# Low parts of an expert's weights on VectorE, two weight chunks loaded earlier, first loads in another order

## The chip, the core and the metric

The kernel runs on one core of one Trainium2 chip. The metric is the device time of one execution in microseconds (us). A core has TensorE (PE: matrix products and transposes), VectorE (DVE), ScalarE (ACT), GpSimd (POOL) and SyncE (SP), each with its own instruction queue that runs in order. Queues meet at semaphores. SyncE issues nearly all loads here; a load stands in SyncE's queue until its buffer is free, and everything behind it stands with it.

## The reference

Three stages, all in fp32, with 2 batches of 768 rows, 8 heads of 64:

```python
# 1: windowed attention, 8 global and 96 local columns, with a slope per head
scores = scale * (q @ k.T) + bias; scores = where(keep, scores, -1e9)
x = softmax(scores) @ v                       # (2, 768, 512)
# 2: a mixture of 8 experts, one expert for each row
logits = x @ w_gate; gate = sigmoid(x @ w_local)
e = argmax(logits) if s == 0 or gate < 0.5 else expert of the row before
out = p[e] * (relu(x @ w1[e]) @ w2[e])        # w1: 512x1024, w2: 1024x512 for each expert
# 3: a mix with the row before
xk = mu_k*x + (1-mu_k)*x_prev;  xr = mu_r*x + (1-mu_r)*x_prev
k = relu(xk @ w_k);  r = sigmoid(xr @ w_r);  out = r * ((k*k) @ w_v)
```

## The kernel before, in words

Each fp32 product is made of three matrix products of rounded halves: an operand is split into a high part, `hi = round(x)`, written by ScalarE, and a low part, `lo = x - hi`, and TensorE adds `hi*hi + lo*hi + hi*lo` (`mm3`, which the trace shows as L598 to L600). So every weight chunk of 128x1024 numbers passes through a load, two ScalarE copies (`whi`) and a subtraction (`wlo`).

The order of the instructions on every engine is that of the Python code; nothing is scheduled by a planner. Hand-written tables say how many steps of a background queue run behind each foreground step.

*Attention.* At the start the two integers `n_global` and `n_local` are loaded (`scalars_load`, L136), cast (L141), and turned into one mask and distance table for each head (`table`, L518; heads above 3 on GpSimd), popped from a list `tq`. Then the pairs of heads run in a pipeline: scores (`emit_qk`, L734), the row minimum (`emit_min`, L746, which needs the tables), the exponential (`emit_exp`, L756), transposes, products with `v`. Dummy products (`warm`, L896) fill some of TensorE's gaps.

*Routing* runs beside the last heads and in a tail after them: gate logits, the switch `ab` (L187 to L211), products that spread it over a row (L221), a scan over the rows (`er`, L232), the sort by expert (L241 to L260), and scatters of the rows from GpSimd into the tensor `xs` (L253). The first expert's work on the rows known early (`fill`, a generator) is the foreground of that tail. Its weights are split by `w_hi(0, c)` and `w_lo(0, c)`, called from `w_next` in between. For chunks 4 to 6 the low part is one GpSimd instruction of 128x1024 (L567), for chunk 7 half of it is on VectorE (L571).

*Experts 1 to 7.* Raw weight chunks live in a ring of four buffers (`wraw`), which x0, the rows of the first expert's later tile, also shares. While the first expert ends, chunks 0 and 1 of expert 1 are loaded and split (`w1q`). From chunk 2 on, loads come from a list `lq`: after each low part (`w_lo_all`, L591) `pump` issues the next load of the list. Token tiles (`x_load`, tiles `xn`, L1120) are in the same list, before the weight chunk with number 7.

*Stage 3's weights* arrive as words that VectorE has to decode. `dec_load` (L1171) loads one piece of 512 KB into one of two `dw` buffers on SyncE's queue; `dec` decodes it in four VectorE steps (L449, L452, L454, L456). The generator `background` runs these steps between the experts' own. Stage 3 follows at about 354 us.

Of the kernel before, what the change touches and what calls it, by code (L numbers as in the profile page):

```python
# [52 lines left out]
class Net:  # L53
# [76 lines left out]
    def scalars_load(self, c):  # L130
        nc = self.nc
        self.raw = raw = c.tile([P, 4], I32, name="n_raw")
        for j, nm in enumerate(("n_global", "n_local")):
            src = self.i[nm].bitcast(I32)
            src = bass.AP(tensor=src.tensor, offset=src.offset, ap=[[0, P], [1, 2]])
            nc.sync.dma_start(out=raw[:, 2 * j:2 * j + 2], in_=src)  # L136

    def scalars(self, c):
        nc, raw = self.nc, self.raw
# [360 lines left out]
    def tables0(self, keep, pool):  # L500
        nc = self.nc
        r0 = self.rel[:, CP:W]
        m0 = pool.tile([P, P], F32, name="m0")
        d0 = pool.tile([P, P], F32, name="d0")
        nc.vector.tensor_scalar(m0, self.colg, self.ng, NEG, op0=ALU.is_ge, op1=ALU.mult)
        nc.vector.tensor_scalar(d0, r0, self.nl, None, op0=ALU.min)
        nc.vector.scalar_tensor_tensor(m0, r0, self.nl, m0, op0=ALU.is_ge, op1=ALU.mult)
        self.tb0 = keep.tile([P, H, P], F32, tag="tb0", bufs=1, name="tb0")

        return [lambda h=h: self.table(self.tb0[:, h, :], d0, m0, h, h > 3) for h in range(H)]  # L510

    def table(self, dst, dist, mask, h, pool):
        nc, s = self.nc, 2.0 ** -(h + 1)
# [19 lines left out]
def build(ctx, tc, ins, out):  # L533
# [21 lines left out]
    def w_hi(r, c):  # L555
        raw = raws[r, c]
        hi = wp.tile([P, 1024], F32R, tag="whi", bufs=10, name=f"whi{r}_{c}")
        for s in range(2):
            sl = slice(s * 512, s * 512 + 512)
            nc.scalar.activation(out=hi[:, sl], in_=raw[:, sl], func=ACTF.Copy)  # L560
        whl[r, c] = hi

    def w_lo(r, c, pool_lo=False):
        raw, hi = raws.pop((r, c)), whl[r, c]
        lo = wp.tile([P, 1024], F32R, tag="wlo", bufs=10, name=f"wlo{r}_{c}")
        if pool_lo:
            nc.gpsimd.tensor_tensor(lo, raw, hi.bitcast(F32), op=ALU.subtract)  # L567
        else:
            for s, eng in ((0, nc.vector), (1, nc.gpsimd)):
                sl = slice(s * 512, s * 512 + 512)  # L570
                eng.tensor_tensor(lo[:, sl], raw[:, sl], hi[:, sl].bitcast(F32), op=ALU.subtract)  # L571
        whl[r, c] = (hi, lo)

    def w_hi1(r, c, s, dve=False):
# [14 lines left out]
    def w_lo_all(r, c):  # L589
        hi, lo = whl[r, c]  # L590
        nc.vector.tensor_tensor(lo, raws.pop((r, c)), hi.bitcast(F32), op=ALU.subtract)  # L591

    def w_split(r, c, pool_lo=False):
        w_hi(r, c)
        w_lo(r, c, pool_lo)

    def mm3(out_, ah, al, bh, bl, first, last):
        nc.tensor.matmul(out_, lhsT=ah, rhs=bh, start=first, stop=False)  # L598
# [126 lines left out]
    def emit_qk(pair):  # L725
        t, h = pair
        j = t % NT
        p = h // 2
        c0 = 0 if j else CP
        N = W - c0  # L730
        k0 = cols(t) + P - N
        ps = [n.bank("S", 2) for _ in range(2)]
        for a in range(2):
            nc.tensor.matmul(ps[a][:, 0:N], lhsT=qz[t % 2][a * HD:(a + 1) * HD, p, :], rhs=strip[a * HD:(a + 1) * HD, p, k0:k0 + N], start=True, stop=True)  # L734
        Ss[pair] = ps
# [144 lines left out]
            step(mid=early_start)  # L880

    with tc.manual_schedule():
        for g in range(2):
            load("k", 0, g)
            load("q", 0, g)
            if g == 0:
                n.scalars_load(n.const)
        n.setup()
        peb = [ap.tile([P, 2 * P], F32, name=f"peb{i}") for i in range(4)]
        qz = [ap.tile([P, PAIRS, P], F32, name=f"qz{i}") for i in range(2)]  # L890
# [3 lines left out]
        def warm(k, m=512):  # L894
            for _ in range(k):
                nc.tensor.matmul(n.bank("O", 2)[:, 0:m], lhsT=n.warm[:, 0:P], rhs=n.warm[:, 0:m], start=True, stop=True)  # L896
# [6 lines left out]
        n.scalars(n.const)  # L903
        tq = n.tables0(ap, tp) + n.tables(ap, tp)
        first = first_half(0)
        for _ in range(9):
            tq.pop(0)()
        for nm, a in ("k1", "q1", "v0", "v1"):
            load(nm, int(a))
# [45 lines left out]
        wseq = []  # L955
        for c in range(NIN, 8):
            wseq.append(lambda c=c: w_hi(0, c))
            wseq.append(lambda c=c: w_lo(0, c, c < 7))

        def w_next():  # L960
            if wseq:
# [4 lines left out]
        first_half(1)  # L966
        del kn[0], qn[0]
        emit_min(0, pairs[0])
        emit_qk(pairs[1])
        warm(NDUM[1], 64)  # L970
        for i in range(NP_ + 3):
            t, h = pairs[i] if i < NP_ else (NTT + (i - NP_) // 4, 2 * ((i - NP_) % 4))
# [119 lines left out]
        for k, _ in enumerate(fl):  # L1092
            if k > 6 and w1q:
                c, s = w1q.pop(0)
                if s < 2:
                    w_hi1(1, c, s)
                else:
                    w_lo1(1, c, s - 2)
    astack.close()
    zp = wstack.enter_context(tc.tile_pool(name="zp", bufs=1))  # L1100
    mstack = ExitStack()
# [288 lines left out]
    with tc.manual_schedule():  # L1390
        lq = []

        for r in range(1, E):
            if r == 1:
                lq.append(lambda r=r: x_load(r))
            else:
                lq.append(lambda r=r: ereg(r))
            for c in range(0 if r > 1 else 2, 8):
                if c == 7 and r < E - 1:
                    lq.append(lambda r=r: x_load(r + 1))  # L1400
                lq.append(lambda r=r, c=c: w_load(r, c))

        def pump(m=1):
            for _ in range(m):
                if lq:
                    lq.pop(0)()

        sq = [(r, c, s) for r in range(1, E) for c in range(0 if r > 1 else 2, 8) for s in range(3)]
        sq += [(E, c, s) for c in WORD for s in range(4)]

        def w3_split(c, s):
            if s == 0:
                w_hi1(E, c, 0)
                return
            if s == 1 and c in DVEHI:
                nc.vector.tensor_copy(whl[E, c][0][:, 512:], raws[E, c][:, 512:])
            elif s == 1:
                w_hi1(E, c, 1)
            else:
                w_lo1(E, c, s - 2)  # L1420

        def W_(m=1):
            for _ in range(m):
                if sq:
                    r, c, s = sq.pop(0)
                    if r == E:
                        w3_split(c, s)
                    elif s < 2:
                        w_hi1(r, c, s)
                    else:  # L1430
                        w_lo_all(r, c)
                        pump(1 if c != 5 else 3)

        pump(1)
        dec_load(PIECES[0])
        pump(1)
        dec_load(PIECES[1])
        pump(1)
        hn = ztile([P, 2, D], F32, "hn")
        eh = [xtile([P, KF, P], c, f"eh{c}") for c in "hl"]  # L1440
        for u in xs_tile(0, xhl0[:, 0], xhl0[:, 1], [hn[:, s, :] for s in range(2)], eh, BASES[0] + 2 * P):
            W_(W0[u])
            B_(B0[u])
            if u == 0:
                pump(1)
            if u in X1_AT:
                x_hi(1, X1_AT.index(u))
            if u - 1 in X1_AT:
                x_lo(1, X1_AT.index(u - 1))
        for r in range(1, E - 1):  # L1450
            nx = len(TILES[r + 1])
            for f in range(KF):
                l1m(r, f)
                if f in (3, 4, 5) and f - 3 < nx:
                    x_lo(r + 1, f - 3)
                if f in (2, 3, 4) and f - 2 < nx:
                    x_hi(r + 1, f - 2)
                W_((1, 2, 2, 1, 1, 1, 1, 1)[f])
                B_(BL1[f])
            nt = len(TILES[r])  # L1460
            for i in range(nt):
                ps = n.bank("O", 2)
                m = nrow(r, i)
                if i == 2:
                    src, a = [tuple(h[:, f, 0:m] for h in h3["hl"]) for f in range(KF)], 0
                else:
                    src, a = [hs[r, f] for f in range(KF)], i
                for f in l2_mm(r, ps, a, src, m):
                    if f == 0 and i == 0:
                        W_(2)  # L1470
                    elif (f < 6 if i else nt < 3 and f < 7):
                        W_(1)
                    if f % 2 == 0:
                        B_(1)
                y_out(rp, ps, BASES[r] + TILES[r][i] * P, m)

        r = E - 1
        for i in range(2):
            hn = wp.tile([P, 2, D], F32, tag="wraw", bufs=4, name=f"hn{i}")
            eh = [xtile([P, KF, P], c, f"eh{c}{i}") for c in "hl"]  # L1480
            xh, xl = (x[:, :, i * P:(i + 1) * P] for x in xhl[r])
            for u in xs_tile(r, xh, xl, [hn[:, s, :] for s in range(2)], eh, BASES[r] + i * P):
                if i:
                    early(u)
                W_(W7[i][u])
                B_(1)
            if i == 0:
                for _ in bg:
                    pass
                n.small_w3(rp)  # L1490
                early(-1)
        stage3()
# [214 lines left out]
```

## Time and profile before

| | before |
|---|---|
| median of three runs | 551.25 us (551.23 to 552.83) |
| profiled execution | 555.6 us, its span 553.8 us |
| TensorE busy | 530.4 us, 96% |
| VectorE busy | 372.8 us, 67% |
| ScalarE busy | 289.5 us, 52% |
| GpSimd busy | 149.1 us, 27% |
| mean granted clock | 0.973 of full |

The span is the time from the first to the last instruction that the profiler saw. Times of single instructions are all from this one execution. A row of a timeline has the start in us, the duration in us, the engine, the line of the kernel, the operation with its output and inputs, and a count; in brackets stands the idle time of the engine just before it and what ended it. TensorE is nearly always busy, so a saving on another engine counts only where TensorE stands behind it. The granted clock of 1.0 stands for 2.4 GHz and 0.5 for 1.2 GHz.

### The profile page before, as it was taken

The numbers are of one execution on the slowest core, as the hardware profiler recorded it, in microseconds if no ns is written. First come the engines' busy times: TensorE is split into PE (matmuls) and PEld (weight loads), VectorE is DVE, ScalarE is ACT, GpSimd is POOL, SyncE is SP. The second block draws the span as 40 slices with busy tenths as digits, with TensorE's granted clock in tenths as the row PEclk, the third lists the DMA queues.
The fourth block names the chain that finished last, engine by engine and source line by source line (L and its number), as shares of the span: only waits on it lengthen the run. The fifth ranks groups of instructions, "written<-read, shape, count | busy, mean of one in ns | idle before, by whom it ended". The sixth has DMA issues, their size and how long they took to land.

```text
span 553.8 us, 9727 instructions
## 1 busy us (share of the span) xinstructions
PE 530.4 (96%) x3285; PEld 450.9 (81%) x3285; DVE 372.8 (67%) x937; ACT 289.5 (52%) x709; POOL 149.1 (27%) x234
## 2 busy tenths in 40 slices
PE   6999999989789799999999999999999999999995
PEld 4787887777668698889898998778898989898885
DVE  6688889786663388588989979869744344444311
ACT  4787888866424544556565655557433332424130
POOL 4443353473530000000000000043535261716130
PEclk9799999987989999999999999999999999999999
DMA  6875374833114984758789897211101010110101
GB/s 127 209 168 144 76 169 105 239 103 126 41 39 141 315 289 154 283 181 273 251 301 339 286 354 247 89 59 57 58 20 43 34 40 38 39 40 1 39 2 43
DMA packets 74137, 76.99 MB, mean 139 GB/s; under 512 B 50496, under 2 KB 50752, under 8 KB 74080
## 3 DMA queue, kind: packets, MB, share of 16 engines
q1 hardware_dynamic: 68464, 63.28, 37.5%
q0 software_dynamic: 1920, 6.29, 3.5%
q10 hardware_dynamic: 3696, 6.72, 3.2%
q8 instruction: 28, 0.46, 0.3%
q14 instruction: 29, 0.24, 0.2%
HBM read 63.27 MB, written 13.01 MB: 138 GB/s over the span
## 4 chain that ended last, share of the span: by engine, by line
PE 69%; DVE 18%; DMA 5%; issue 3%; ACT 2%; SPq 1%; POOL 0%; DVEq 0%; ACTq 0%; POOLq 0%
PE O L598 10%; PE O L600 9%; PE O L599 9%; PE S L598 6%; PE S L600 6%; PE S L599 6%; PE S L734 4%; DVE wlo L591 4%; DMA wraw<-in_moe_w_dram 3%; PE PT L600 3%; PE PT L599 3%; PE PT L598 3%; PE T L680 2%; PE R L181 2%; PE PT L765 2%
## 5 line engine op out<-in xcount | busy, mean ns | idle before, releaser
L582 ACT ACTIVATE whi<-wraw 128x512 fp32r<-128x512 f32 x116 | 67.2, 623 | 18.8 <-DMA wraw<-in_moe_w_dram 11.5
L591 DVE TENSOR_TENSOR wlo<-wraw,whi 128x1024 fp32r<-128x1024 f32 x54 | 65.8, 1219 | 11.4 <-ACT whi L582 11.2
L1270 ACT ACTIVATE rl<-S 128x256 f32<-128x256 f32 x48 | 18.5, 385 | 80.4 <-PE S L600 80.3
L598 PE MATMUL S<-xkh,whi 128*128 128x256 f32 x192 | 54.5, 284 | 0.4 <-DVE sq L1272 0.4
L599 PE MATMUL S<-xkl,whi 128*128 128x256 f32 x192 | 53.6, 279 | 0.6 <-DVE xkl L1248 0.6
L600 PE MATMUL S<-xkh,wlo 128*128 128x256 f32 x192 | 53.6, 279 | 0.0
L1280 POOL TENSOR_TENSOR kl<-sq,kh 128x256 fp32r<-128x256 f32 x40 | 31.9, 807 | 80.2 <-ACT kh L1279 80.2
L1225 POOL MEMSET strip<- 128x4 f32 x2 | 0.2, 115 | 192.4 <-DVE wlo L587 192.4
L1310 DVE TENSOR_TENSOR o<-O,sig 128x512 f32<-128x512 f32 (+1 forms) x13 | 8.5, 651 | 61.3 <-PE O L600 34.5
L746 DVE CUSTOM_DVE_ANT_0 sc<-S,tb 128x232 f32<-128x232 f32 (+1 forms) x96 | 32.3, 373 | 21.0 <-PE S L734 14.1
L756 ACT ACTIVATE peb<-sc,nm 128x232 f32<-128x232 f32 (+1 forms) x96 | 44.2, 464 | 1.9 <-DVE nm L746 1.9
L598 PE MATMUL O<-whi,kh 128*128 128x512 f32 (+1 forms) x104 | 39.2, 377 | 0.0
L599 PE MATMUL O<-wlo,kh 128*128 128x512 f32 (+1 forms) x104 | 39.2, 377 | 0.0
L600 PE MATMUL O<-whi,kl 128*128 128x512 f32 (+1 forms) x104 | 39.2, 377 | 0.0
L598 PE MATMUL O<-whi,hh 128*128 128x512 f32 x96 | 38.0, 396 | 0.0
L599 PE MATMUL O<-wlo,hh 128*128 128x512 f32 x96 | 37.9, 395 | 0.0
L600 PE MATMUL O<-whi,hl 128*128 128x512 f32 x96 | 37.9, 395 | 0.0
L775 ACT ACTIVATE pth<-PT 128x512 fp32r<-128x512 f32 (+1 forms) x48 | 26.9, 561 | 20.5 <-PE PT L767 15.2
L1272 DVE SCALAR_TENSOR_TENSOR sq<-S,rl 128x256 f32<-128x256 f32 x48 | 19.9, 420 | 25.8 <-ACT rl L1270 25.0
L599 PEld LDWEIGHTS S<-xkl,whi 128*128 128x128 f32 x192 | 36.1, 188 | 1.0 <-DVE xkl L1248 0.8
L598 PEld LDWEIGHTS S<-xkh,whi 128*128 128x128 f32 x192 | 36.0, 187 | 0.9 <-DVE sq L1272 0.6
L734 PE MATMUL S<-strip,qz 64*128 64x232 f32 (+1 forms) x192 | 33.7, 419 | 2.9 <-DVE nm L746 2.8
(351 smaller groups left out, 1607.7 us busy)
## 6 DMA issues: line engine op xcount, KB each, us to landing
wraw<-in_moe_w_dram SPq DMA_DIRECT2D x64, 512.0 KB, 5.2
ys<-yo ACTq DMA_DIRECT2D x17, 256.0 KB, 4.1
dw<-in_moe_w_k_dram SPq DMA_DIRECT2D x8, 512.0 KB, 4.9
dw<-in_moe_w_v_dram SPq DMA_DIRECT2D x8, 512.0 KB, 5.7
xn<-xs SPq DMA_DIRECT2D x14, 256.0 KB, 5.7
vn<-in_v_dram SPq DMA_DIRECT2D x12, 256.0 KB, 4.0
kn<-in_k_dram SPq DMA_DIRECT2D x11, 256.0 KB, 4.5
qn<-in_q_dram SPq DMA_DIRECT2D x11, 256.0 KB, 3.2
```

The costliest lines, as they stand in the source:

```text
L582: nc.scalar.activation(out=whl[r, c][0][:, sl], in_=raws[r, c][:, sl], func=ACTF.Copy)
L591: nc.vector.tensor_tensor(lo, raws.pop((r, c)), hi.bitcast(F32), op=ALU.subtract)
L598: nc.tensor.matmul(out_, lhsT=ah, rhs=bh, start=first, stop=False)
L599: nc.tensor.matmul(out_, lhsT=ah, rhs=bl, start=False, stop=False)
L600: nc.tensor.matmul(out_, lhsT=al, rhs=bh, start=False, stop=last)
L734: nc.tensor.matmul(ps[a][:, 0:N], lhsT=qz[t % 2][a * HD:(a + 1) * HD, p, :], rhs=strip[a * HD:(a + 1) * HD, p, k0:k0 + N], start=True, sto ...
L746: nc.vector.tensor_tensor_reduce(out=sc[:, c0:W], in0=ps[a][:, 0:W - c0], in1=(n.tb if t % NT else n.tb0)[:, h + a, :], scale=1.0, scalar= ...
L756: nc.scalar.activation(out=pe[:, PAD + c0:2 * P], in_=sc[:, c0:W], func=ACTF.Exp, scale=-1.0, bias=nm[:, h + a:h + a + 1], accum_out=sm[:, ...
L775: nc.scalar.activation(out=hi[:, 0:ps.shape[1]], in_=ps, func=ACTF.Copy)
L1270: nc.scalar.activation(out=rl, in_=ps[:, 0:TB], func=ACTF.Relu)
L1272: nc.vector.scalar_tensor_tensor(sq_, ps[:, 0:TB], 0.0, rl, op0=ALU.max, op1=ALU.mult)
L1280: (nc.gpsimd if b else nc.vector).tensor_tensor(hl, sq_, hh.bitcast(F32), op=ALU.subtract)
```

## The change

*The start.* `n_global` becomes the first load of SyncE's queue and `n_local` the first of ScalarE's. The head tables are made in the order 0, 1, 4, 5, 6, 7, 2, 3; only six are made before the first half of the second tile, and three list entries (tables 2 and 3 and the global one) follow after the first row minimum, with one dummy product of 512 columns ahead of the second pair's scores.

*The low parts of the first expert.* `w_lo` has no GpSimd part any more: the low parts of chunks 4 to 7 are whole VectorE instructions of 128x1024. (`w_split` was not called.)

*Two weight chunks.* In the loop over the rest of `fill`, behind each of the two low parts of expert 1's chunks 0 and 1, chunks 2 and 3 are loaded. The list `lq` of expert 1 therefore starts at chunk 4, and every later load comes out of it two pumps earlier.

```diff
-            nc.sync.dma_start(out=raw[:, 2 * j:2 * j + 2], in_=src)
+            (nc.scalar if j else nc.sync).dma_start(out=raw[:, 2 * j:2 * j + 2], in_=src)
...
-        return [lambda h=h: self.table(self.tb0[:, h, :], d0, m0, h, h > 3) for h in range(H)]
+        return [lambda h=h: self.table(self.tb0[:, h, :], d0, m0, h, h > 3) for h in (0, 1, 4, 5, 6, 7, 2, 3)]
...
-    def w_lo(r, c, pool_lo=False):
+    def w_lo(r, c):
         raw, hi = raws.pop((r, c)), whl[r, c]
         lo = wp.tile([P, 1024], F32R, tag="wlo", bufs=10, name=f"wlo{r}_{c}")
-        if pool_lo:
-            nc.gpsimd.tensor_tensor(lo, raw, hi.bitcast(F32), op=ALU.subtract)
-        else:
-            for s, eng in ((0, nc.vector), (1, nc.gpsimd)):
-                sl = slice(s * 512, s * 512 + 512)
-                eng.tensor_tensor(lo[:, sl], raw[:, sl], hi[:, sl].bitcast(F32), op=ALU.subtract)
+        nc.vector.tensor_tensor(lo, raw, hi.bitcast(F32), op=ALU.subtract)
         whl[r, c] = (hi, lo)
...
     with tc.manual_schedule():
+        n.scalars_load(n.const)
         for g in range(2):
             load("k", 0, g)
             load("q", 0, g)
-            if g == 0:
-                n.scalars_load(n.const)
...
-        for _ in range(9):
+        for _ in range(6):
             tq.pop(0)()
...
-            wseq.append(lambda c=c: w_lo(0, c, c < 7))
+            wseq.append(lambda c=c: w_lo(0, c))
...
         emit_min(0, pairs[0])
+        warm(1)
         emit_qk(pairs[1])
+        for _ in range(3):
+            tq.pop(0)()
         warm(NDUM[1], 64)
...
                     w_lo1(1, c, s - 2)
+                if s == 3:
+                    raws.pop((1, c))
+                    w_load(1, c + 2)
...
-            for c in range(0 if r > 1 else 2, 8):
+            for c in range(0 if r > 1 else 4, 8):
```

VectorE's queue in the last routing step, before: from the flag `fl` over the switch `ab` (L211) and the scan `er` to the one-hot rows `oh`; `wlo0_7` is the low part of chunk 7 of expert 0.

```order
L198 TENSOR_SCALAR fl10_2356<-LS_295 128x2
L207 SCALAR_TENSOR_TENSOR eq10_2358<-eq10_2358,iota_e_94 128x16
L210 TENSOR_REDUCE fr10_2371<-eq10_2358 128x2
L211 SCALAR_TENSOR_TENSOR ab10_2355<-fr10_2371,fl10_2356 128x2
L167 TENSOR_TENSOR X11_2379<-T_240_2374,RI_296 128x512
L607 TENSOR_TENSOR etb0_2286<-PT_241_2384,etb00_2285 128x512
L232 SCALAR_TENSOR_TENSOR er10_2406<-R_242_2391,er8_2206,br10_2396 1x256
L571 TENSOR_TENSOR wlo0_7_2412<-wraw0_7_2168,whi0_7_2403 128x512
L243 TENSOR_SCALAR oh10_2417<-R_243_2415,iota_p_96 8x256
```

The same place with the change:

```order
L198 TENSOR_SCALAR fl10_2358<-LS_297 128x2
L566 TENSOR_TENSOR wlo0_5_2367<-wraw0_5_1991,whi0_5_2346 128x1024
L207 SCALAR_TENSOR_TENSOR eq10_2360<-eq10_2360,iota_e_94 128x16
L210 TENSOR_REDUCE fr10_2373<-eq10_2360 128x2
L211 SCALAR_TENSOR_TENSOR ab10_2357<-fr10_2373,fl10_2358 128x2
L167 TENSOR_TENSOR X11_2381<-T_241_2376,RI_298 128x512
L598 TENSOR_TENSOR etb0_2288<-PT_242_2386,etb00_2287 128x512
L566 TENSOR_TENSOR wlo0_6_2403<-wraw0_6_2076,whi0_6_2369 128x1024
L232 SCALAR_TENSOR_TENSOR er10_2408<-R_243_2393,er8_2208,br10_2398 1x256
L566 TENSOR_TENSOR wlo0_7_2414<-wraw0_7_2170,whi0_7_2405 128x1024
L243 TENSOR_SCALAR oh10_2418<-R_244_2416,iota_p_96 8x256
```

Three low parts of 128x1024 now stand between `fl` and `oh`, in place of one of 128x512.

SyncE's queue at the first expert's end, before: from the last token tile of expert 1 (`xn1_2`) on; `wraw1_2` is chunk 2 of expert 1, `dw16` and `dw17` are pieces of stage 3's weights.

```order
L1120 DMA xn1_2_2670<-xs_63 80x512
L1171 DMA dw16_2682<-in_moe2_w_r_dram 128x1024
L549 ISA
L549 DMA wraw1_2_2684<-in_moe_w1_dram 128x1024
L1171 DMA dw17_2686<-in_moe2_w_r_dram 128x1024
L549 ISA
L549 DMA wraw1_3_2688<-in_moe_w1_dram 128x1024
```

With the change, from the load of `x0` on:

```order
L1083 DMA x0_2524<-xs_63 128x512
L549 ISA
L549 DMA wraw1_2_2601<-in_moe_w1_dram 128x1024
L1114 TENSOR_LOAD rowi_2498
L1114 ISA x2
L549 ISA
L549 DMA wraw1_3_2628<-in_moe_w1_dram 128x1024
L1116 ISA
L1116 DMA xn1_0_2651<-xs_63 128x512
```

Chunks 2 and 3 of expert 1 moved from behind the three token tiles `xn1_0` to `xn1_2` to a place right behind `x0` and ahead of `xn1_0`.

SyncE's queue in expert 5's weight loads, before: chunks 1 to 4 and the piece `dw6`.

```order
L549 DMA wraw5_1_3942<-in_moe_w1_dram 128x1024
L549 ISA
L549 DMA wraw5_2_4000<-in_moe_w1_dram 128x1024
L1171 DMA dw6_4042<-in_moe2_w_k_dram 128x1024
L549 ISA
L549 DMA wraw5_3_4063<-in_moe_w1_dram 128x1024
L551 ISA
L551 DMA wraw5_4_4093<-in_moe_w2_dram 128x2x512
```

With the change, chunks 2 to 4 and the pieces `dw5` and `dw6`:

```order
L549 DMA wraw5_2_3892<-in_moe_w1_dram 128x1024
L1167 DMA dw5_3924<-in_moe2_w_k_dram 128x1024
L549 ISA
L549 DMA wraw5_3_3947<-in_moe_w1_dram 128x1024
L551 ISA
L551 DMA wraw5_4_4005<-in_moe_w2_dram 128x2x512
L1167 DMA dw6_4047<-in_moe2_w_k_dram 128x1024
```

`dw6` stood between chunks 2 and 3 of expert 5, and now stands behind chunk 4. The same holds for the pieces around it.

## Rows read from the trace of the kernel before

**Rows 1.** Page, part 1: busy time, share of the span, instructions.

```profile
PE 530.4 (96%) x3285; PEld 450.9 (81%) x3285; DVE 372.8 (67%) x937; ACT 289.5 (52%) x709; POOL 149.1 (27%) x234
```

**Rows 2.** Windows: busy us of each engine, granted clock, DMA share, GB/s.

```profile
11.90:22.10 10.20, 10.13 (x42) 7.63 (x42) 7.82 (x37) 5.64 (x23) 6.22 (x16) 0.50 0.89 203
...
155.00:158.40 3.40, 3.40 (x9) 2.09 (x9) 3.03 (x6) 1.57 (x3) 1.60 (x1) 0.52 0.00 0
...
192.60:196.00 3.40, 3.40 (x10) 2.62 (x9) 3.40 (x7) 1.71 (x4) 0.00 (x0) 0.51 0.87 298
```

**Rows 3.** Timeline of VectorE and TensorE at the start.

```profile
5.89 0.17 DVE L141 CAST n_f<-n_raw 128x4 f32<-128x4 int32 x1 [3.36 <-DMA n_raw<-in_n_local_dram]
...
7.54 1.16 DVE L518 SCALAR_TENSOR_TENSOR tb<-d,m 128x128 f32<-128x128 f32 x4
...
10.31 0.29 DVE L746 CUSTOM_DVE_ANT_0 sc<-S,tb 128x128 f32<-128x128 f32 x1 [0.37 <-PE S L734]
...
6.12 0.49 PE L734 MATMUL S<-strip,qz 64*128 64x128 f32 x4
...
9.79 0.69 PE L734 MATMUL S<-strip,qz 64*128 64x128 f32 x4 [2.32 <-DVE nm L746]
```

**Rows 4.** Timeline of VectorE, GpSimd and TensorE in the routing tail.

```profile
148.88 5.21 DVE L211 SCALAR_TENSOR_TENSOR ab<-fr,fl 128x2 f32<-128x2 f32 x1
...
148.43 0.96 POOL L253 DMA_INDIRECT xs<-X,posi  x1 [2.74 <-DMA xs<-X,posi]
149.41 4.64 POOL L567 TENSOR_TENSOR wlo<-wraw,whi 128x1024 fp32r<-128x1024 f32 x2
...
154.14 0.38 PE L221 MATMUL R<-ident,ab 128*1 128x128 f32 x2 [4.37 <-DVE ab L211]
...
159.57 0.61 PE L260 MATMUL R<-ident,mm 8*128 8x8 f32 x4
```

**Rows 5.** Page, part 5: one low part of 128x1024 on VectorE (busy, mean ns).

```profile
L591 DVE TENSOR_TENSOR wlo<-wraw,whi 128x1024 fp32r<-128x1024 f32 x54 | 65.8, 1219 | 11.4 <-ACT whi L582 11.2
```

**Rows 6.** Chain of waits (start, us, what) and TensorE's timeline, first expert's end.

```profile
181.83 6.25 DMA wraw<-in_moe_w_dram
...
190.28 0.50 PE L598 MATMUL O<-whi,ehh 128*128 128x512 f32 x1 [1.75 <-ACT ehh L606]
...
192.25 0.50 PE L600 MATMUL O<-whi,ehl 128*128 128x512 f32 x1 [1.24 <-DVE ehl L607]
```

**Rows 7.** Window of experts 4 to 7, and TensorE's waits at its end.

```profile
262.00:353.00 91.00, 90.79 (x559) 80.52 (x558) 82.81 (x141) 53.66 (x108) 0.00 (x0) 1.00 0.81 287
...
PE O L600 <- DVE ehl L607: 0.7, 1, 0.7
```

**Rows 8.** Timeline of SyncE's load issues, experts 4 to 7.

```profile
265.67 0.39 SPq L551 DMA_DIRECT2D wraw<-in_moe_w_dram  x1
...
289.58 0.38 SPq L551 DMA_DIRECT2D wraw<-in_moe_w_dram  x1
...
318.70 2.10 SPq L1120 DMA_DIRECT2D xn<-xs  x2
...
339.65 0.38 SPq L551 DMA_DIRECT2D wraw<-in_moe_w_dram  x1
```

**Rows 9.** Timeline of VectorE: first decode step of a `dw` piece.

```profile
268.13 0.69 DVE L449 CUSTOM_DVE_ANT_0 w<-dw 128x512 f32<-128x512 f32 x1
...
292.36 0.68 DVE L449 CUSTOM_DVE_ANT_0 w<-dw 128x512 f32<-128x512 f32 x1
...
321.97 0.68 DVE L449 CUSTOM_DVE_ANT_0 w<-dw 128x512 f32<-128x512 f32 x1
...
343.47 0.68 DVE L449 CUSTOM_DVE_ANT_0 w<-dw 128x512 f32<-128x512 f32 x1
```

**Rows 10.** Tile views: `dw` from 262 to 353; the `wraw` issued 0.59 after a `dw`.

```profile
DMA to landing us min/median/max: 3.5/5.7/6.8
...
DMA to landing us min/median/max: 4.7/4.7/4.7
```

More of the change, by code (lines that the diff above doesn't have):

```diff
@@ L591, in w_lo_all @@
         nc.vector.tensor_tensor(lo, raws.pop((r, c)), hi.bitcast(F32), op=ALU.subtract)
-    def w_split(r, c, pool_lo=False):
-        w_hi(r, c)
-        w_lo(r, c, pool_lo)
     def mm3(out_, ah, al, bh, bl, first, last):
```

## The prediction

> **What bounds the kernel now.** I read the page's busy times first: TensorE works 530.4 of 553.8 us [rows 1], so only the places where it stands still or runs slowly can give anything. The windows at half clock came next. In the stretches of [rows 2] the granted clock is about 0.5, the lower of the two levels (1.2 GHz); each stands at a place where TensorE had just waited. Then I read the timelines around the three places that the diff touches: the start, the last step of routing, and the first expert's end. At the start VectorE idles 3.36 us for the two scalars, and TensorE waits 2.32 us for the first row minimum [rows 3]. In the routing tail a VectorE instruction of 128x2 numbers lasts 5.21 us, and TensorE waits 4.37 us for it [rows 4]. At the first expert's end a weight chunk lands 6.25 us after its issue, and TensorE, behind ScalarE and VectorE, waits 1.75 and 1.24 us for it [rows 6]. Last I read the stretch from 262 to 353 us, which the edits do not name but whose SyncE queue they reorder: TensorE is busy in 90.79 of 91 us there, VectorE in 82.81 [rows 7].
>
> The sum is made against the profiled execution, 555.6 us (span 553.8 and 1.8 around it). That is 4.35 above the median of 551.25; I carry the difference over to the median. What a measurement of this kernel can tell from no change is about 0.3%, 1.65 us.
>
> **Start: a gain of 1.4, and 1.2 by the clock.** The scalars' cast starts at 5.89 after 3.36 us of waiting. Of its two loads the second goes from SyncE's fourth place to the first of ScalarE's queue, and the first to the head of SyncE's, so I expect the cast about 1.6 earlier. Before the first minimum two fewer VectorE tables (1.16 for four [rows 3], so 0.6) and the global base (about 0.8 of the gap from the last table to the minima) stand. The first minimum then waits for its scores instead, which TensorE starts at 6.12 for 0.49 [rows 3]; the first key load now starts one issue later, some 0.4, so I place it at 7.0. Two tables and the base (1.4) and its own work (0.4) put the second pair's minimum at 8.9, against 10.31: gain 1.4. Its upper bound is the 1.6 of the loads, the lower one nothing, if the key load is then late by what the scalars are early. The added 512-column dummy matmul lies in the 2.32 us that TensorE waits. The half-clock stretch from 11.90 to 22.10 follows directly: if the shorter wait before it removes it, VectorE's 7.82 busy us are the next limit of those 10.20, so at most 2.4 are gained; if not, 0. I take the middle, 1.2.
>
> **Routing tail: 3.3.** `ab` starts at 148.88, and its end, 154.09, is that of the two GpSimd low parts, 154.05 [rows 4]. They go to VectorE, one in front of `eq`, one in front of the scan, one behind it, and an earlier one in a wait for a gate result. A low part takes 1.219 there [rows 5]. One of them before `ab`: it ends at about 150.3 instead of 154.09, 3.8 earlier. One and a half more before the sorting matmul L260 (the last chunk already had half of its columns on VectorE) cost 1.8; but TensorE no longer works off its own rows at half clock in between (3.40 us at 0.52, [rows 2], half of which, 1.7, falls away). Together L260 is at about 156.3 instead of 159.57: 3.3. Upper bound 3.8; lower bound: if the 5.21 are not caused by GpSimd, three low parts are added to the chain and nothing is taken away, a loss of 3.7.
>
> GpSimd is in its scatter from 148.43, and `ab` waits from 148.88 through it and both low parts [rows 4]. The Trainium skill, "SBUF — State Buffer", section "Who interferes with whom", says that a VectorE instruction with two SBUF inputs and a GpSimd one that reads SBUF exclude each other for a whole instruction; the rows agree. By it the new low part, which has two SBUF inputs, would still wait for the scatter's 0.96 to end, and the tail would give 2.5 instead of 3.3. I leave the sum at 3.3, since that is within its bounds.
>
> **First expert's end: 4.7.** The chunk (1,2) is issued at 181.83 and lands 6.25 later [rows 6]. In the new order its load stands directly behind that of x0, before the three token loads, and waits only for the low part of the last chunk of expert 0; it lands well before its use. Then TensorE's two waits go, 1.75 + 1.24 = 3.0; the half clock that follows (3.40 us at 0.51, [rows 2]) goes with them, 1.7. What is late next is nothing that I see: TensorE is dense from 196 on. Bounds: 4.7 and, if the token loads behind two more weight loads become the new wait, about 0. VectorE has nothing to do with the time that it wins there, since it soon waits for TensorE's products again.
>
> These gains are 1.4 + 1.2 + 3.3 + 4.7 = 10.6.
>
> **What is given back: the decode loads.** From here on every weight load stands two places earlier in SyncE's queue, but its buffer is one of four and is freed by the same low part as before. So SyncE stands longer at each, and what is queued behind it waits: the 512 KB `dw` loads of the stage-3 weights, which VectorE decodes (L449) in order, with its low parts behind. Before, the load for the use at 292.36 was ahead of the weight load issued at 289.58; now it is behind it, 0.55 later. In the rows that is 2.78 us before the use [rows 8, 9], and no `dw` lands in less than 3.5 (median 5.7 in this stretch, [rows 10]). Eight uses between 268.13 and 343.47 are such pairs; the first has 268.13 - 265.67 = 2.46, the last 343.47 - 339.65 = 3.82, and all eight together 25.56. With a landing of L after its issue they stall VectorE by 8 x (0.55 + L) - 25.56. A ninth, used at 321.97, comes behind the two token loads of 318.70 (2.10 for both, [rows 8]), so at 320.9: L - 1.1. The other uses have over five us, or none lost.
>
> L is not in the trace for this order. A load alone takes 3.5, the second of a pair 4.7, the median is 5.7 [rows 10]. I take 4.3: the weight load ahead has stood at its gate, so little else is in flight, but it shares the way with `dw`. Stall: 8 x 4.85 - 25.56 + 3.2 = 16.4. VectorE has 91.00 - 82.81 = 8.2 of idle time [rows 7], of which 7.6 lies behind the first such use and takes up part. The rest, 8.8, reaches the end of the stretch, and there TensorE already waits 0.7 for VectorE's low part [rows 7]: it has no lead left, so the lateness goes on to the end. Bounds: at L = 3.5 the stall is 9.6 and 2.0 are given back; at 5.7 it is 29.0 and 21.4.
>
> **Sum.** -10.6 + 8.8 = -1.8: 555.6 becomes 553.8 in the profiled execution, and the median 551.25 - 1.8 = 549.4.
>
> **Rivals.**
> - *The gains stay whole.* If the `dw` loads land in 3.5 or less, or if VectorE gets ahead of TensorE and so issues the gates earlier against the uses, nothing or 2.0 is given back: 540.7 to 542.7. For it: the lone landing of 3.5. Against it: VectorE has only 9% of idle time in that stretch to get ahead with.
> - *Slower by the decode loads.* The same mechanism, at the same place, 265 to 352 us. From L = 4.5 on the stall eats the whole gain (9 x 4.5 - 22.3 - 7.6 = 10.6). At the pair's 4.7 the time is 553.1, at 5.0 it is 555.8, at the median of 5.7 about 562. For it: 4.7 is the row that is closest in form. Against it: the median comes from moments with more loads in flight. I give 555.8.
> - *The tail does not shorten.* If `ab` waits for something other than GpSimd's low parts, the tail costs 3.7 instead of giving 3.3, and with the rest as above the time is 549.4 + 7.0 = 556.4. Against it: the two ends agree within 0.04.
> - *The start gives nothing,* because the scalars land as late on the other queue and the clock falls again: 549.4 + 2.6 = 552.0, no change that can be told.
>
> **How the numbers follow.** My forecast has a chance of 0.46; its own range, by L from 3.9 to 4.5, is 545.9 to 551.3. Gains whole 0.13, slower by the decode loads 0.27, the tail 0.05, the start 0.09. Of the forecast 0.35 is faster by over 0.3%, 0.10 within it, 0.01 slower; the gains whole are faster; of the slower decode case 0.24 is slower and 0.03 within; the tail is slower; of the start 0.05 within, 0.04 slower. Sum: faster 0.48, same 0.18, slower 0.34. The range 541.5 to 556.5 leaves out 0.1 on each side.
>
> **What would show it.** Start: the second pair's minimum near 8.9, and the clock behind it. Tail: `ab` at 0.16 and no wait of L221 on it. First expert: no wait of `whi` on a weight load near 185, and no clock at half behind it. Decode: idle time of VectorE before L449, put down to the `dw` load, near 16 us in about nine places; if that is under 5, I am wrong on the give-back, and if it is over 20 the kernel is slower. Also wrong would be a VectorE that reaches the stretch's end late while TensorE does not wait for it.

## The result: slower by half a per cent, with the profile after

| | before | changed |
|---|---|---|
| median of 20 runs | 553.74 us (551.23 to 559.74) | 557.57 us (554.95 to 560.11) |
| ratio | | 1.0058, 95% interval 1.0034 to 1.0082 |
| profiled execution, span | 555.6, 553.8 | 557.42, 555.6 |

I had forecast 549.4 from a median of 551.25 that came from three runs; over 20 runs the median of the kernel before is 553.74. The forecast had the wrong sign. It is the second rival, slower by the decode loads, that happened.

Two measures split the trace in two: when TensorE starts the first product of expert 1 (the first that reads `xl`, the low part of its rows), and how long it takes from there to the first transposes of stage 3 (`yg`). Both come from tile views, whose rows name the first and last start. Here are the rows before:

```profile
L599 PE MATMUL S<-xl,whi x96: 278/279/318, 196.4 to 331.9; 128*128 128x256 f32 x80, 128*128 128x336 f32 x16
...
L1220 PE MATMUL R<-ident,yg x24: 270/272/300, 367.2 to 495.3; 128*128 128x128 f32 x24
```

The same tiles after:

```profile
L590 PE MATMUL S<-xl,whi x96: 276/279/318, 185.4 to 328.0; 128*128 128x256 f32 x80, 128*128 128x336 f32 x16
...
L1216 PE MATMUL R<-ident,yg x24: 270/272/300, 368.9 to 497.3; 128*128 128x128 f32 x24
```

At the first product of expert 1 the changed kernel is 11.0 us ahead (196.4 to 185.4). At the first `yg` it is 1.7 behind (367.2 to 368.9). The experts took 183.5 instead of 170.8, so 12.7 were given back. The windows of these two stretches show what TensorE did in them (its busy time stands first behind the length; ahead of DMA share and GB/s stands the granted clock). Before:

```profile
196.40:367.20 170.80, 170.08 (x1034) 150.61 (x1034) 141.03 (x272) 96.82 (x199) 2.06 (x3) 1.00 0.72 248
```

After:

```profile
185.40:368.90 183.50, 173.13 (x1035) 151.80 (x1034) 142.07 (x273) 96.77 (x200) 2.06 (x3) 0.99 0.69 232
```

TensorE was idle 10.37 us instead of 0.72, which is 9.65 of the 12.7. The other 3.05 are longer busy time for the same products. TensorE's waits after, in the same stretch (us in total, times, longest):

```profile
PE O L591 <- DVE ehl L598: 4.5, 1, 4.5
PE R L1130 <- DMA xn<-xs: 2.5, 1, 2.5
PE S L589 <- DVE hl L1155: 2.0, 2, 1.1
PE S L591 <- DVE wlo L586: 1.4, 1, 1.4
```

The first line is the 0.7 of [rows 7], grown to 4.5; it comes last. The waits for `hl` and `wlo`, 3.3 us, come before it, from 272 to 326 us, and so does that for the token tiles `xn`. Two of the earlier ones and the last, in TensorE's timeline:

```profile
272.55 0.38 PE L589 MATMUL S<-xh,whi 128*128 128x256 f32 x1 [0.85 <-DVE hl L1155]
...
318.67 0.39 PE L591 MATMUL S<-xh,wlo 128*128 128x256 f32 x1 [1.36 <-DVE wlo L586]
...
353.63 0.52 PE L591 MATMUL O<-whi,ehl 128*128 128x512 f32 x1 [4.55 <-DVE ehl L598]
```

The clock fell right behind the last one, as the window from 353 us on shows (0.62):

```profile
353.00:357.00 4.00, 3.37 (x11) 2.74 (x12) 1.75 (x3) 0.68 (x2) 0.00 (x0) 0.62 0.00 0
```

And VectorE's waits from 255 to 353 us, all of them, are waits for decode loads, 18.7 us in ten places:

```profile
DVE w L449 <- DMA dw<-in_moe_w_k_dram: 10.2, 4, 2.9
DVE w L449 <- DMA dw<-in_moe_w_v_dram: 8.5, 6, 3.0
```

One of them in full, the load that the prediction took as its example [rows 8, 9]. SyncE's issues, and then VectorE's timeline:

```profile
281.99 0.38 SPq L551 DMA_DIRECT2D wraw<-in_moe_w_dram  x1
282.42 0.46 SPq L1167 DMA_DIRECT2D dw<-in_moe_w_k_dram  x1
...
284.17 0.69 DVE L456 SCALAR_TENSOR_TENSOR w<-dw,w 128x512 uint32<-128x512 uint32 x1
287.54 0.69 DVE L449 CUSTOM_DVE_ANT_0 w<-dw 128x512 f32<-128x512 f32 x1 [2.67 <-DMA dw<-in_moe_w_k_dram]
```

VectorE would have used it at 284.87, 2.88 after the weight load's issue (2.78 in [rows 8, 9]). It was issued 0.43 behind that weight load and took 5.1 to land, so VectorE stood 2.67.

### The profile page after: what moved, and what is told of

Same layout as the page of the kernel before. It is cut to its first block, busy times and chain, and to the rows that moved or that the text cites. A ratio compares the mean times of both kernels' runs of the same rounds, so it can differ in the third digit from the quotient of the medians.

```text
span 555.6 us, 9728 instructions
## 1 busy us (share of the span) xinstructions
PE 528.9 (95%) x3287; PEld 447.9 (81%) x3287; DVE 373.6 (67%) x940; ACT 289.2 (52%) x709; POOL 141.8 (26%) x230
## 4 chain that ended last, share of the span: by engine, by line
PE 69%; DVE 15%; DMA 9%; issue 3%; ACT 1%; SPq 1%; POOL 0%; DVEq 0%; ACTq 0%; POOLq 0%
PE O L589 9%; PE O L591 9%; PE O L590 8%; PE S L589 6%; PE S L591 6%; PE S L590 6%; PE S L725 4%; DMA dw<-in_moe_w_v_dram 4%; DMA dw<-in_moe_w_k_dram 4%; DVE wlo L586 4%; PE PT L591 3%; PE PT L590 3%; PE PT L589 3%; PE T L671 2%; PE R L181 2%
## 5 line engine op out<-in xcount | busy, mean ns | idle before, releaser
L591 PE MATMUL S<-xkh,wlo 128*128 128x256 f32 x192 | 53.7, 279 | 0.0
L591 PE MATMUL O<-whi,kl 128*128 128x512 f32 (+1 forms) x104 | 39.2, 377 | 0.0
L591 PE MATMUL O<-whi,hl 128*128 128x512 f32 x96 | 38.0, 396 | 0.0
L591 PEld LDWEIGHTS S<-xkh,wlo 128*128 128x128 f32 x192 | 36.0, 188 | 0.0
```

The lines of the kernel that those rows point to most:

```text
L591: nc.tensor.matmul(out_, lhsT=al, rhs=bh, start=False, stop=last)
```

## The experiments

The theory: the decode loads come late because they stand in SyncE's queue behind weight loads that wait there for a buffer. The rival: they land late because the loads are denser once the work ahead is shorter, or because of another part of the change, wherever they stand in the queue. The column "experts" is the time from the first product of expert 1 to the first `yg`, read from tile views as above; the clock's changes in attention don't touch it.

| kernel | ratio to before (95%) | starts expert 1 | experts | waits before L449 |
|---|---|---|---|---|
| before | | 196.4 | 170.8 | 1.1 |
| changed | 1.0058 (1.0034 to 1.0082) | 185.4 | 183.5 | 18.7 |
| changed, two empty entries | 0.9839 (0.9782 to 0.9897) | 185.9 | 170.5 | 0.6 |
| changed, one empty entry | 0.9810 (0.9759 to 0.9861) | 190.8 | 171.7 | 8.5 |
| changed, decode loads on GpSimd's queue | 0.9892 (0.9822 to 0.9962) | 187.7 | 170.7 | 5.9 |
| before, list run ahead by two | 1.0213 (1.0154 to 1.0273) | 193.7 | 183.8 | 19.1 |
| before, chunks part alone | 1.0187 (1.0115 to 1.0258) | 191.0 | 185.9 | 20.3 |
| before, chunks part, order kept | 0.9889 (0.9842 to 0.9937) | 189.8 | 169.9 | 0.8 |
| before, start alone | 0.9928 (0.9891 to 0.9966) | 189.4 | 170.7 | 0.7 |
| before, low parts alone | 0.9888 (0.9827 to 0.9949) | 190.7 | 169.9 | 0.5 |

**Two empty entries.** The early loads stay, and all later loads stand where they stood.

```diff
+            if r == 1:
+                lq.extend([lambda: None] * 2)
             for c in range(0 if r > 1 else 4, 8):
```

> The changed kernel with two empty entries at the head of the load list of expert 1, so that chunks 2 and 3 are still loaded early, but every later weight load stands where it stood before against the decode loads. Theory (queue order): the gains stay whole and the waits of VectorE before L449 on a decode load fall from 18.7 us to under 3, so 9 to 11 us faster than the kernel before, ratio 0.980 to 0.984. Rival (a fuller stretch: the decode loads land late since the loads are denser once the work before it is shorter, wherever they stand): the waits stay above 10 us and the time is within 2 us of the changed kernel, ratio 0.998 to 1.006.

It took 545.19 us against 554.09 on the same chip. VectorE's waits from 245 to 345 us:

```profile
DVE hl L1155 <- ACT hh L1154: 5.7, 7, 2.0
DVE wlo L586 <- ACT whi L577: 1.6, 1, 1.6
DVE w L449 <- DMA dw<-in_moe_w_k_dram: 0.6, 1, 0.6
```

The waits for ScalarE's products are back, and those for decode loads are gone. The loads are not less dense than in the changed kernel: the window of this stretch has a DMA share of 0.84 and 292 GB/s, and TensorE without a gap, where the changed kernel has 0.76 and 263 GB/s (first row):

```profile
255.00:353.00 98.00, 88.26 (x530) 76.77 (x528) 78.85 (x134) 52.21 (x103) 0.00 (x0) 1.00 0.76 263
...
251.00:341.00 90.00, 90.00 (x559) 80.30 (x559) 82.16 (x142) 51.93 (x106) 0.00 (x0) 1.00 0.84 292
```

Nor does a decode load land sooner after its issue; over the whole trace it is the changed kernel that has the lower median (5.4, below):

```profile
DMA to landing us min/median/max: 3.5/5.9/6.8
```

So density is out as the cause, and what changed is when a load is issued against its use. The ratio is in the theory's band. The median is the lowest of the study, though the kernel with one empty entry (below) is not told apart from it.

**Decode loads on GpSimd's queue.** The weight loads keep their new places; the decode loads get a queue in which nothing else waits.

```diff
-        nc.sync.dma_start(out=t.rearrange("p a b -> p (a b)"), in_=n.w3_half(w3, i))
+        nc.gpsimd.dma_start(out=t.rearrange("p a b -> p (a b)"), in_=n.w3_half(w3, i))
```

> The changed kernel with the decode loads issued from GpSimd's queue instead of SyncE's; the weight loads keep their new places. They then wait for their own buffer alone. Theory (queue order): waits before L449 under 3 us, ratio 0.978 to 0.985. Rival (the loads land late for lack of DMA time): waits above 10 us and a ratio of 0.998 to 1.006.

The ratio, 0.9892, is above the theory's band (0.978 to 0.985), which its interval (0.9822 to 0.9962) reaches, and below the rival's. The waits are 5.9 us, twice the 3 expected. The landings, minimum, median and maximum in this stretch:

```profile
DMA to landing us min/median/max: 3.8/6.0/8.8
```

Against 3.5/5.7/6.8 of [rows 10], the slowest landing is 2.0 longer. The 5.9 cost nothing visible: the experts took 170.7.

**The list run ahead by two, nothing else.** This was meant as the give-back alone.

```diff
-        pump(1)
+        pump(3)
         dec_load(PIECES[0])
```

> The kernel before with the list of loads run two entries ahead from its start (three entries before the first decode load instead of one), and nothing else of the change: no gain at the start or in the routing tail, and chunk 2 of expert 1 at most a microsecond earlier. Theory (queue order): the give-back alone shows, waits before L449 of 14 to 20 us, 8 to 13 us slower than before, ratio 1.014 to 1.024. Rival (the give-back comes from the other parts, or from a fuller stretch): ratio 0.997 to 1.003.

It took 565.75 us, in the theory's band; the waits (19.1) and the experts' time (183.8) are close to those of the changed kernel. None of the other parts is needed for the loss. One expectation failed: it is not the give-back alone, since from the last L260 to the first product of expert 1 it takes 33.3 us (160.4 to 193.7) instead of 36.5, so that the shift brings some 3 us of the gain at the first expert's end with it.

**The chunks part alone**, the two early loads and the list that starts at chunk 4:

```diff
+                if s == 3:
+                    raws.pop((1, c))
+                    w_load(1, c + 2)
...
-            for c in range(0 if r > 1 else 2, 8):
+            for c in range(0 if r > 1 else 4, 8):
```

> The kernel before with the early loads of chunks 2 and 3 of expert 1 and the shorter list alone. Theory (queue order): about 4.7 us gained at the first expert's end and 12 to 13 given back by the decode loads, so 6 to 9 us slower, ratio 1.010 to 1.017. Rival (the give-back needs the other parts): 4 to 5 us faster, ratio 0.991 to 0.993.

It has the sign of the theory and is above its band. TensorE starts expert 1 5.4 us earlier and the experts take 15.1 longer. Against the changed kernel's 183.5 that is 2.4 more; their granted clock is lower:

```profile
191.00:376.90 185.90, 174.98 (x1033) 153.86 (x1032) 142.34 (x273) 96.51 (x199) 2.06 (x3) 0.97 0.66 229
```

TensorE is busy 174.98 us here for the same products, against 173.13 in the changed kernel, which is 1.85 of the 2.4.

**The same part, order kept**, with two empty entries as in the first experiment:

> The kernel before with the early loads of chunks 2 and 3 of expert 1, and two empty list entries that keep every later load in its place against the decode loads. Prediction of the third part without the give-back: the waits of 1.75 and 1.24 us and the half clock behind them go, 3.0 to 4.7 us faster, ratio 0.9915 to 0.9945. Rival (VectorE or the token loads become the new wait there): ratio 0.998 to 1.002.

As expected, a little more than the band: 550.1 us against 555.79. From the last L260 to the first product of expert 1 it takes 32.4 (157.4 to 189.8) instead of 36.5 (159.9 to 196.4), which is 4.1 of the 4.7 predicted. In the profiled execution another 2.5 us lie ahead of the part, where its code is that of the kernel before (below), and 0.9 in the experts.

**One empty entry**, every later load one place earlier instead of two:

```diff
+            if r == 1:
+                lq.extend([lambda: None] * 1)
             for c in range(0 if r > 1 else 4, 8):
```

> The changed kernel with one empty entry instead of two, so that the later weight loads stand one place earlier than before, not two. Theory (queue order): each decode load then waits for one low part less and gets some 2.3 us more; only the tightest ones are late, waits before L449 of 1 to 6 us, time 1 to 4 us above the kernel with two empty entries, ratio to before 0.983 to 0.992. Rival (the delay is not tied to the place in the queue but comes on as soon as any load moves): 12 us or more above it, ratio 1.003 to 1.010.

The median is 2.0 us above that of two entries, as expected; the ratio, 0.981, is just under its band (0.983 to 0.992), and the waits are above theirs (1 to 6): 8.5 us in eight places.

```profile
DVE w L449 <- DMA dw<-in_moe_w_v_dram: 5.3, 5, 1.9
...
DVE w L449 <- DMA dw<-in_moe_w_k_dram: 3.2, 3, 2.1
```

The experts took 171.7, only 1.2 more than with two entries. Here 8.5 us of stall cost TensorE 1.2; in the changed kernel 18.7 cost 12.7. So about 7 us are free, close to the 7.6 of idle time that the prediction set against the stall, and most of what comes beyond them is paid: by these two rows, 18.7 - 7 = 11.7 against a cost of 12.7 that has half clock in it. The medians of one and two entries were measured beside different medians of the kernel before (555.79 and 554.09). By the ratios one entry is no slower (0.9810 and 0.9839), and the intervals overlap: these runs do not tell the two apart.

**The start alone** (its lines of the diff, and no others):

> The kernel before with the reordered first loads and tables alone. By the prediction 1.4 us at the start and up to 2.4 by the clock, so 1.4 to 3.8 us faster, ratio 0.993 to 0.9975, and the second pair's first row minimum near 9.4 in the profile as in the changed kernel (10.31 before). Rival (the win at the start is lost again before the routing tail, where TensorE waits for VectorE anyway): ratio 0.999 to 1.001 and the last product of the switch ab at the same time as before, 154.2.

The ratio reaches beyond the band's fast end and the second pair's minimum started at 9.62. The rival's sign did not come: the last product of the switch started at 147.4, not at 154.2. More of it is clock than I thought. The window of the first 24 us before, and the same for this kernel:

```profile
0.00:24.00 24.00, 19.78 (x90) 13.53 (x91) 15.74 (x72) 11.67 (x38) 12.05 (x42) 0.79 0.76 160
```

```profile
0.00:24.00 24.00, 20.32 (x119) 13.36 (x120) 18.20 (x83) 14.99 (x48) 12.58 (x43) 1.00 0.86 187
```

No half clock is left here in this execution; in the changed kernel there is still some (0.86), with the same code at the start.

**The low parts alone** (`w_lo` and its call as in the diff):

> The kernel before with the low parts of chunks 4 to 7 of the first expert on VectorE alone. Prediction: the switch instruction takes 0.16 us instead of 5.21, and 2.5 to 3.8 us are gained, ratio 0.993 to 0.9955; TensorE's wait on the switch falls from 4.4 to under 1. Rival (the 5.21 us are not GpSimd's): they stay, and three low parts of 1.22 come on top, 3.7 us slower, ratio 1.007.

The ratio, 0.9888, is beyond the band's fast end (0.993), which its interval reaches. The routing tail gave what was predicted: from `lh` to the last L260 it takes 9.0 us (147.2 to 156.2) instead of 12.7, so 3.7. Another 2.0 came between L260 and the first product of expert 1, and 0.9 in the experts, which I did not expect of this part. TensorE's wait on the switch fell to 0.4, and the switch took 0.16 us:

```profile
148.35 1.22 DVE L566 TENSOR_TENSOR wlo<-wraw,whi 128x1024 fp32r<-128x1024 f32 x1
149.89 0.16 DVE L211 SCALAR_TENSOR_TENSOR ab<-fr,fl 128x2 f32<-128x2 f32 x1
```

The 5.21 us were GpSimd's. The kernel with the start alone, in which GpSimd still makes the low parts, shows it once more, since other instructions met them there. VectorE's and GpSimd's timelines of that kernel:

```profile
141.51 5.15 DVE L197 TENSOR_TENSOR eq<-LS,MX 128x16 f32<-128x16 f32 x1
...
147.12 0.16 DVE L211 SCALAR_TENSOR_TENSOR ab<-fr,fl 128x2 f32<-128x2 f32 x1
...
140.99 0.96 POOL L253 DMA_INDIRECT xs<-X,posi  x1 [2.01 <-DMA xs<-X,posi]
141.98 4.65 POOL L567 TENSOR_TENSOR wlo<-wraw,whi 128x1024 fp32r<-128x1024 f32 x2
```

There `eq`, which also has two inputs in SBUF, is held until 146.66, when GpSimd ends at 146.63, and `ab` is quick.

What stays open: by their ratios the three parts alone (start, low parts, chunks with the order kept) are 0.7, 1.1 and 1.1% faster than the kernel before, 2.9% together, and all three at once (two empty entries) 1.6%. They don't add up. One double count can be seen: from 140 us to the first product of expert 1 the granted clock was 0.94 before and 1.00 with the low parts alone, so that a gain which the prediction booked to the chunks, the half clock behind the first expert's end, came with this part too, though TensorE still waited there (1.3 and 1.2). And the granted clock in a stretch that no part edits differs between executions. In the window from 24 to 140 us it was 0.96 before and 1.00 with the chunks part alone, whose code is the same up to there:

```profile
24.00:140.00 116.00, 112.79 (x822) 90.36 (x821) 93.64 (x357) 91.51 (x286) 49.92 (x74) 0.96 0.56 142
```

```profile
24.00:140.00 116.00, 110.82 (x838) 88.67 (x837) 96.87 (x364) 93.06 (x289) 50.32 (x74) 1.00 0.56 142
```

That is enough to blur single parts of 2 to 5 us, but I did not show that the two together are all of the 1.3%, some 7 us, that are missing.

## Why the prediction was wrong, point by point

The gains were right in sum: 10.6 predicted, 11.0 measured at the first product of expert 1. That they were so close is in part luck, since two terms came out smaller and two larger. By parts, in the profiled executions:

- *Start.* The cast started at 4.97 (5.89 before), 0.9 earlier and not 1.6, and the second pair's minimum at 9.39 (10.31), 0.9 and not 1.4 (7.0 + 1.4 + 0.4 are 8.8, not the 8.9 of the text). The first minimum had to wait for the scores, as said: it started at 7.46. From there on to the last gate step `lh`, which started at 144.3 instead of 147.2, another 2.9 - 0.9 = 2.0 came, where the term for the clock was 1.2. The granted clock of the first 24 us rose from 0.79 (shown above) to 0.86:

```profile
0.00:24.00 24.00, 20.59 (x98) 13.13 (x98) 15.74 (x72) 12.72 (x41) 12.09 (x42) 0.86 0.80 163
```

  That is worth at most 24 x 0.07 = 1.7. The rest lies behind it: from 24 to 140 us the granted clock was 0.96 before and 0.97 after, a stretch that the text did not count and in which executions differ by more than that.
- *Tail.* From `lh` to the last L260 it took 9.0 (144.3 to 153.3) instead of 12.7 (147.2 to 159.9): 3.7, with 3.3 predicted (the terms of the text, 3.8 - 1.8 + 1.7, add up to 3.7 and not to its 3.3, and a full 0.96 less, for the scatter, would have left 2.3 of those, not 2.5). TensorE's wait on `ab` fell from 4.4 to 0.4.
- *First expert.* From the last L260 to the first product 32.1 (153.3 to 185.4) instead of 36.5: 4.4, with 4.7 predicted. No half clock followed.

The step that failed is the size of the give-back, 8.8, which was 12.7. Its mechanism was that of the text, down to the loads: piece by piece in the two timelines, the nine decode loads that it counts are the nine that newly stalled VectorE, 17.5 us together (the tenth stall, 1.25 at 349.22, had been 0.41 before). The path was that of the text only in part. The text lets the lateness reach the end of the stretch and stop TensorE there. TensorE stood 4.55 there, 3.3 for VectorE in three places before it, and 2.5 for token loads. In the sum two terms were wrong, and the second, which the sum did not have, is the larger: TensorE stood 9.65 more instead of 8.8, and beside that it was busy 3.05 longer.

- *The landing, 4.3.* I took a value between the lone load and the second of a pair, on the argument that little else is in flight. The decode loads of the changed kernel took 4.4 at the least, with a median of 5.4:

```profile
DMA to landing us min/median/max: 4.4/5.4/7.0
```

  The example's 5.1 is above the pair's second, 4.7, that I had called the row closest in form and then set aside, and the nine took 4.95 on average (to the use that waited, where a landing is not recorded). The stall came to 18.7, 17.6 more than before, where I had 16.4. That it was not further off is luck: with 4.95 the formula of the text gives the nine 9 x 4.95 - 22.3 = 22.3, and they stalled 17.5, since they had 4.8 us more lead in all than in the trace before. What absorbed it was well sized: VectorE's waits for `hh` and `whi` in the experts fell from 11.9 and 6.1 to 7.8 and 2.4, that is 7.8 us, where I had 7.6. The difference, 9.8, is 1.0 above the 8.8 and close to TensorE's 9.65 of new idle time, in which the 2.5 for token loads are counted too.
- *Longer busy time of TensorE, not in the sum at all.* I had counted the half clock as a gain wherever a wait of TensorE goes, and did not count it as a loss where one comes. Behind the wait of 4.55 before L591 at 353.63 it came back:

```profile
350.00:360.00 10.00, 6.37 (x23) 5.14 (x24) 7.68 (x12) 2.32 (x5) 0.10 (x1) 0.83 0.00 0
```

  Ten us at 0.83 are 1.7 lost, and before and behind them the granted clock of the experts is 1.00. So the clock is 1.7 of the 3.05. The other 1.3 fell at full clock, and what they are stays open.

Then -11.0 + 12.7 = +1.7 at the first `yg`, and +1.8 in the span. The medians are 3.8 apart and the ratio says 0.6%, 3.2 us; the profiled execution of the kernel before was 1.9 above its own median, and that of the changed one at its.

The chances were also off. With the break-even at a landing of 4.5 and the nearest row at 4.7, the slower case was the likelier one by my own sum, and I had given it 0.27. The sign that I had set for it, idle time over 20 before L449, did not come (18.7), and the kernel was slower all the same. The other three rivals can be dropped: the gains were not whole, the tail did shorten, and the start gave something. The token loads, which I had bounded only at the first expert, did become a wait, 2.5 us at 296.60 for `xn`; they too stand in SyncE's queue behind weight loads, and with the order kept (two empty entries) that wait is gone.

## What to carry to other kernels

When a load is pulled forward in a queue that runs in order, look at what it now stands in front of, not only at who waits for it. Here the weight loads stood at their buffers as before, the decode loads stood behind them, and moving only the list ahead made the experts 13.0 us longer (183.8 against 170.8). Placeholders in the list (two lines here) keep the early loads and the old order, and turned a ratio of 1.0058 (1.0034 to 1.0082) into one of 0.9839 (0.9782 to 0.9897).

Here a stall of an engine off the critical path was free up to about its idle time behind it (some 7 of 91 us) and nearly full price after that; where TensorE then waited, the clock cost 1.7 more.

## What the runs showed of the hardware that I had not expected

- The holding works the other way too. In the routing tail VectorE's `ab` had been held by GpSimd. With a low part on VectorE ahead of it, GpSimd's scatter took 1.84 us instead of the 0.98 of the kernel with the start alone, while the one that met no low part took 0.96. GpSimd's timeline of the kernel with the low parts alone, after which VectorE's low part beside it:

```profile
142.48 1.84 POOL L253 DMA_INDIRECT xs<-X,posi  x1 [11.75 <-DVE cnt L298]
146.60 0.96 POOL L253 DMA_INDIRECT xs<-X,posi  x1 [2.28 <-DMA xs<-X,posi]
...
142.26 1.20 DVE L566 TENSOR_TENSOR wlo<-wraw,whi 128x1024 fp32r<-128x1024 f32 x1
```

  The low part ends at 143.46, and the scatter 0.86 later. The Trainium skill, "SBUF — State Buffer", section "Who interferes with whom", says that of a VectorE instruction and a GpSimd one that need the shared ports the first to issue has them for its whole instruction and the other stands; these rows agree. The case that the prediction weighed by it, the second low part against the scatter before it, did not come up in the changed kernel: that scatter was over 1.05 us before the low part began (144.40 and 145.45).
- A held instruction shows as busy, not as waiting: the 5.21 us of `ab` and the 5.15 of `eq` stand in VectorE's busy time, with no releaser named.
- The granted clock of one code differs between executions, 0.96 and 1.00 from 24 to 140 us, without a change in what TensorE was given to do.
